# A two-stage kernel (decayed linear attention, then maxout): units of 256 tokens on 128 partitions, y made channel-first, and an order written out as a table

## The chip, the cores and the metric

The kernel runs on one core of a Trainium2 chip. The metric is device time in microseconds of that core; a kernel is run three times and the median counts.

## The reference

Four batches, eight heads, 768 tokens, 48 channels a head. A state of 48x48 a head is decayed by w and gains the outer product of k and v at each token; y reads it with r, with a bonus u for the token itself. The heads are then laid side by side (384 channels) and go through two products to 1024, an elementwise maximum, and a product back to 384. Everything is float32 at the boundary.

```python
for t in range(S):
    kt, vt, rt, wt = (k[:, :, t], v[:, :, t], r[:, :, t], w[:, :, t])
    cur = np.einsum('bhd,bhe->bhde', u[None] * kt, vt)
    y[:, :, t] = np.einsum('bhd,bhde->bhe', rt, state + cur)
    state = wt[:, :, :, None] * state + np.einsum('bhd,bhe->bhde', kt, vt)
...
x = np.ascontiguousarray(attn_out.transpose(0, 2, 1, 3)).reshape(B * S, H * D)
h1 = x @ w1
h2 = x @ w2
g = np.maximum(h1, h2)
return (g @ w_out).astype(np.float32)
```

## The kernel before

The tokens are cut into twelve units of 2 batches by 128 tokens. A unit's 64 token pairs of one batch lie on 64 partitions and those of the other batch on the other 64; the two tokens of a pair (index i) lie side by side along the free dimension. `load` brings w, k, r and v of a unit with eight transfers of 64 partitions (line 77), each piece 384 bytes long (2 tokens of 48 float32), into a pool of four buffers.

For each unit, `logw` takes the logarithm of w and adds the two tokens of a pair (POOL, line 172); `cumsum` makes the exclusive running sum over pairs with a product by a triangular matrix in float32 (line 198); `exps` gives the decay up to each token (A) and its inverse (iA); `scale_rk` multiplies r and k by them; `transp` turns both channel-first through TensorE (line 238) and copies them from PSUM on DVE (line 243). `scores` multiplies turned k by turned r in 64-row tiles (line 293) and a mask takes the causal half (line 296). `kv`, `decay` and `decay_exp` carry the state from one chunk to the next; the decay of the whole chunk makes a round trip through DRAM on ACT's queue (lines 216 and 224), because it has to change from the free dimension to partitions. `y_inter` adds the bonus (line 308) and the state's part (line 315), `y_intra` the chunk's own part (line 328). y comes out with tokens on partitions; `xt` turns it channel-first through TensorE (line 340).

The maxout is folded: max(h1, h2) = (h1 + h2)/2 + |h1 - h2|/2. `weights` makes wd = w1 - w2, and wc = (w1 + w2) @ w_out/2 once. `gate` computes x @ wd (line 352), ACT takes the absolute value (line 356), and `outp` adds x @ wc (line 364) and |x @ wd| @ w_out/2 (line 367), copies the 128x384 result (line 370) and sends it out on SP's queue (line 373) with a destination in which the pair index i is the outermost dimension.

The order is written out by hand in `step(a, t, m)`: in one step three units are in work, unit a in its sums and exponentials, unit t in its attention products, unit m in the maxout. The engines run their instructions in the order of issue. Ahead of step n, `load(n + 2)` is issued on SP, behind the two stores of the step before. The first three units and the weights come before the steady part.

## Time and profile before

| | us |
|---|---|
| median of 3 runs | 226.78 |
| the runs | 226.43 to 228.17 |
| span of the profiled execution | 226.8 |
| PE busy | 159.0 |
| DVE busy | 114.1 |
| POOL busy | 113.6 |
| ACT busy | 91.7 |

The profile was taken on one execution, and its span agrees with the median. 28.9 MB move through the DMA engines in it, nearly all on SP's queue. The profile names instructions by line: PE is TensorE's products, PEld its weight loads, SPq the issuing of transfers by SP. A "chain" is the work that ended last, followed back from the end of the span. A window row has, after its bounds and length, the busy time and count of PE, PEld, DVE, ACT and POOL, then the granted TensorE clock, the DMA share (1.00 is all 16 engines busy with one packet each, and packets overlap a little, so that it can be above 1), and GB/s. A chain row has the start, the length and what it is.

### The profile page before, as it was taken

What the parts mean: (1) busy time and instruction counts of PE and PEld (TensorE: products, weight loads), DVE (VectorE), ACT (ScalarE), POOL (GpSimd) and SP (SyncE); (2) the same over time, 40 slices, a digit from 0 to 9 for tenths busy, and PEclk for the clock granted to TensorE, in tenths of its full rate; (3) what the DMA queues carried; (4) which work ended last, traced back from release to release, by engine and by line L of the source; (5) the groups of instructions that cost most, each with busy time, mean ns of one, the idle gap of its engine ahead of it and who ended that gap; (6) DMA issues with size and microseconds to landing.
All of it is one profiled execution on the core that took longest, in us unless ns stands there. A gap on an engine that the chain in (4) does not pass through costs nothing.

```text
span 226.8 us, 5085 instructions
## 1 busy us (share of the span) xinstructions
PE 159.0 (70%) x2104; PEld 104.3 (46%) x2104; DVE 114.1 (50%) x135; ACT 91.7 (40%) x159; POOL 113.6 (50%) x118
## 2 busy tenths in 40 slices
PE   0216557195799848898839898378888398988910
PEld 0014444153576634666615656236556156665600
DVE  5166878710969490185840785802858405660000
ACT  2233113303765613464433556035644347344500
POOL 8494750004788828638549179086295494300000
PEclk9999999999999995899976999959999679999975
DMA  6979999990296439539584485385385811111110
GB/s 128 211 113 217 406 356 134 198 152 0 66 150 129 104 104 172 133 76 151 141 163 104 100 169 117 101 158 132 85 143 146 177 49 50 53 52 31 48 42 35
DMA packets 66254, 28.91 MB, mean 127 GB/s; under 512 B 61220, under 2 KB 65444, under 8 KB 66232
## 3 DMA queue, kind: packets, MB, share of 16 engines
q1 hardware_dynamic: 55792, 28.51, 55.0%
q10 hardware_dynamic: 10440, 0.08, 2.7%
q8 instruction: 16, 0.26, 0.5%
q14 instruction: 6, 0.05, 0.1%
HBM read 23.83 MB, written 4.76 MB: 126 GB/s over the span
## 4 chain that ended last, share of the span: by engine, by line
DMA 20%; PE 16%; SPq 8%; ACT 5%; issue 2%; DVE 1%; POOL 0%; ACTq 0%; DVEq 0%
DMA lw<-in_w_dram 20%; PE go L367 6%; SPq L77 6%; PE go L352 3%; PE go L364 3%; SPq L373 2%; ACT gT L356 2%; PE sc L293 1%; PE y L328 1%; ACT xT L342 1%; ACT osb L370 1%; ACT lw L170 1%; DVE kT L243 1%; PE y L315 1%; PE y L308 1%
## 5 line engine op out<-in xcount | busy, mean ns | idle before, releaser
L172 POOL TENSOR_TENSOR lp<-lw 128x384 f32<-128x384 f32 x12 | 12.3, 1022 | 60.5 <-ACT lw L170 39.5
L367 PE MATMUL go<-wo_sb,gT 128*128 128x384 bf16 x192 | 40.8, 362 | 0.0
L352 PE MATMUL go<-xT,wd_sb 128*128 128x256 bf16 x288 | 37.2, 273 | 2.5 <-ACT xT L342 1.5
L296 DVE TENSOR_TENSOR M<-sc,mask 128x1024 bf16<-128x1024 f32 x24 | 29.3, 1221 | 8.4 <-PE sc L293 8.4
L364 PE MATMUL go<-wc_sb,xT 128*128 128x384 bf16 x72 | 19.0, 381 | 18.7 <-ACT gT L356 18.7
L352 PEld LDWEIGHTS <-wd_sb 128*128 128x128 bf16 x288 | 26.9, 98 | 10.3 <-issue 5.5
L243 DVE COPY rT<-tr 128x1024 bf16<-128x1024 bf16 x12 | 8.3, 688 | 45.8 <-PE tr L238 45.8
L356 ACT ACTIVATE gT<-go 128x512 bf16<-128x512 f32 x48 | 27.3, 588 | 5.6 <-PE go L352 5.4
L370 ACT COPY osb<-go 128x384 f32<-128x384 f32 x24 | 11.5, 478 | 43.3 <-PE go L367 43.3
L367 PEld LDWEIGHTS <-gT 128*128 128x128 bf16 x192 | 20.7, 108 | 16.7 <-issue 6.7
L198 PE MATMUL ex<-lp,tri 128*128 128x384 f32 x24 | 12.1, 592 | 19.5 <-POOL lp L172 14.8
L180 POOL TENSOR_TENSOR rku<-rku,u_b 128x768 f32<-128x768 f32 x12 | 22.4, 1863 | 0.9
L179 POOL TENSOR_TENSOR rku<-lr,lk 128x768 f32<-128x768 f32 x12 | 22.4, 1868 | 0.0
L189 POOL TENSOR_TENSOR vd<-lv,dg 128x768 bf16<-128x768 f32 x12 | 17.7, 1474 | 9.1 <-DVE dg L187 8.3
L170 ACT ACTIVATE lw<-lw 128x768 f32<-128x768 f32 x12 | 10.1, 842 | 29.2 <-DMA lw<-in_w_dram 29.2
L203 DVE TENSOR_TENSOR mz<-ex,lw 128x384 f32<-128x384 f32 x12 | 6.7, 557 | 27.9 <-ACT A L202 27.9
L238 PE MATMUL tr<-ident,rkn 128*128 128x128 bf16 x192 | 16.3, 234 | 4.3 <-DVE rkn L230 3.0
L364 PEld LDWEIGHTS <-xT 128*128 128x128 bf16 x72 | 6.5, 105 | 23.0 <-issue 21.0
L238 PEld LDWEIGHTS <-rkn 128*128 128x128 bf16 x192 | 13.6, 105 | 7.0 <-DVE rkn L230 4.4
L231 DVE TENSOR_TENSOR rkn<-lk,iA 128x768 bf16<-128x768 f32 x12 | 16.0, 1333 | 0.0
L230 DVE TENSOR_TENSOR rkn<-lr,A 128x768 bf16<-128x768 f32 x12 | 15.5, 1293 | 0.3 <-ACT A L209 0.2
L333 ACT CAST x<-y 128x768 bf16<-128x768 f32 x12 | 9.6, 798 | 13.1 <-PE y L328 12.9
(56 smaller groups left out, 215.2 us busy)
## 6 DMA issues: line engine op xcount, KB each, us to landing
lw<-in_w_dram SPq DMA_DIRECT2D x24, 192.0 KB
lk<-in_k_dram SPq DMA_DIRECT2D x24, 192.0 KB
lr<-in_r_dram SPq DMA_DIRECT2D x24, 192.0 KB
lv<-in_v_dram SPq DMA_DIRECT2D x24, 192.0 KB
out_dram<-osb SPq DMA_DIRECT2D x24, 192.0 KB
w1f<-in_moe_w_dram SPq DMA_DIRECT2D x1, 1536.0 KB
w2f<-in_moe_w_dram SPq DMA_DIRECT2D x1, 1536.0 KB
wof<-in_moe_w_out_dram SPq DMA_DIRECT2D x1, 1536.0 KB
```

The lines of the kernel that those rows point to most:

```text
L179: nc.gpsimd.tensor_mul(rku, L[n]["r"], L[n]["k"])
L180: nc.gpsimd.tensor_mul(byi(rku), byi(rku), u_b.rearrange("p (h d) -> p h d", h=H).unsqueeze(1).to_broadcast([P, 2, H, D]))
L189: nc.gpsimd.tensor_mul(byi_inv(vd), L[n]["v"], dg.to_broadcast([P, H, 2, D]))
L230: nc.vector.tensor_mul(rkn[:, 0, :, :, 0:D], byi(L[n]["r"]), s["A"])
L231: nc.vector.tensor_mul(rkn[:, 1, :, :, 0:D], byi(L[n]["k"]), s["iA"])
L238: nc.tensor.transpose(tp[:, p, :, i, :], s["rkn"][:, x, i, 2 * p:2 * p + 2, :].rearrange("s r d -> s (r d)"), ident)
L296: nc.vector.tensor_mul(M.rearrange("s e p t -> s (e p) t"), sc.rearrange("s e p t -> s (e p) t"), mask[:, i].rearrange("s i q -> s (i q)") ...
L352: nc.tensor.matmul(g[:, f, :], wd_sb[:, ko, fo * P:(fo + 1) * P], s["xT"][:, ko].rearrange("p j t -> p (j t)"), start=(f == 0 and ko == 0) ...
L356: nc.scalar.activation(s["gT"][:, 2 * j:2 * j + 2].rearrange("p f j t -> p f (j t)"), g, AF.Abs)
L364: nc.tensor.matmul(o, s["xT"][:, ko, b, :], wc_sb[:, ko, :], start=(ko == 0), stop=False)
L367: nc.tensor.matmul(o, s["gT"][:, fo, b, :], wo_sb[:, fo, :], start=False, stop=(fo == FO - 1))
L370: nc.scalar.copy(osb, o)
```

## The change

The tokens are cut into segments of 256 tokens of one batch: 128 token pairs on 128 partitions. A unit is one or two batches of such a segment: two units of one batch first, then five of two batches, seven in all. One product by the triangle makes the running sum over all 128 pairs of a batch (line 272); w of a pair is multiplied before the logarithm (`wp`), so that one logarithm and one exponential a batch are taken, and the missing factor of w goes into r and k by multiplications (`rw`, `kw`). Scores are still made in tiles of 64 rows, q being the half of the 128 pairs; the state has two places, one for each half. y is made channel-first: the state, the values and the bonus are the stationary operands (lines 452, 464 and 474, the first two in pieces of 32 columns) and tokens run along the free dimension, so that y goes from PSUM straight to xT. The maxout is folded with a relu in place of the absolute value: wd = w1 - w2, wc = w2 @ w_out, max(h1, h2) = h2 + relu(h1 - h2). The gate's products have 512 columns where a unit has two batches. The row of decays makes its round trip on SP's queue. A 128x384 result goes out as two transfers of 64 rows. The weights come in ten pieces through five staging buffers. The loops are replaced by a table, ORDER, one word an operation; a letter after @ names the engine (a for ACT, d for DVE, p for POOL).

```diff
+UNITS = ((0, 1, 0), (1, 1, 0), (2, 2, 0), (0, 2, 1), (2, 2, 1), (0, 2, 2), (2, 2, 2))
...
+ORDER = """
+zero.v.0 tri load.0.w ident zero.m zero.r sel load.0.k zero.s.0 zero.k.1 mask load.0.r zero.v.1
+zero.v.2 u load.0.v zero.s.1 wp.0@d wload.1.0 zero.k.0 ln.0 wload.0.0 wload.1.1 ex.0 wload.0.1
+wload.1.2 rk.0.0@p mz.0 e0.0 ie.0 row.0 ru.0.0@p kw.0@d vb.0.0@a scale.0.1.0@d vb.0.1@p w2cast.0@p
+wdiff.0@d tr.0.1.0 w2turn.0 te.0.1.0@a dg.0 wload.0.2 w2cast.1@p woload.0 kv.0 w2take.0@d w2turn.1
+wdiff.1@d w2take.1@a vd.0.0@d wl.0 woload.1 woload.2 w2cast.2@d wdiff.2@d w2turn.2 wocast.0@p
+w2take.2@a rw.0@d woload.3 load.1.w scale.0.0.0@d we.0 st.0.0 tr.0.0.0 wocast.1@a load.1.k st.0.1
+...
+sc.3.0.0 te.3.1.1@a op.2.2 st.3.1 vd.3.0@p mk.3.0.0 load.5.r sb.3.0@a rk.4.0@p vd.3.1@d tr.3.0.1
+sb.3.1@a sc.3.0.1 op.2.0 te.3.0.1@a wl.4 rk.4.1@p we.3 oe.2.2@a mk.3.0.1 load.5.v sc.3.1.0 oe.2.0@a
+op.2.1 vb.4.0@a mk.3.1.0 ru.4.0@p vb.4.1@a sc.3.1.1 op.2.3 sm.3@d os.2.0 os.2.2 wp.5@p oe.2.1@d
+yi.3.0 oe.2.3@a mk.3.1.1 os.2.1 ya.3.0.0 we.4 ya.3.0.1 rw.4@p ln.5 yb.3.0 kw.4@d yi.3.1 xe.3.0@a
+ya.3.1.0 os.2.3 yb.3.1 ya.3.1.1 scale.4.0.0@p ex.5 xe.3.1@a vb.5.0@a ru.4.1@d load.6.w gt.3.0 e0.5
+vb.5.1@p tr.4.0.0 rl.3.0@a gt.3.1 scale.4.1.0@p te.4.0.0@d gt.3.2 rl.3.1@a mz.5 rl.3.2@a gt.3.3
+gt.3.4 rl.3.3@a scale.4.1.1@p dg.4 tr.4.1.0 rl.3.4@a gt.3.5 gt.3.6 scale.4.0.1@p ie.5 load.6.k
+rl.3.5@d tr.4.1.1 te.4.1.0@d rl.3.6@a gt.3.7 kv.4 te.4.1.1@a rl.3.7@d rk.5.0@p sc.4.0.0 st.4.0
+...
+mk.6.1.0 yi.6.0 yb.6.0 oe.5.1@d ya.6.0.1 ya.6.0.0 os.5.1 yi.6.1 xe.6.0@d yb.6.1 ya.6.1.1 ya.6.1.0
+op.5.2 xe.6.1@a gt.6.0 oe.5.2@a os.5.2 gt.6.1 rl.6.0@a rl.6.1@a gt.6.2 gt.6.3 rl.6.2@a rl.6.3@a
+gt.6.4 gt.6.5 rl.6.4@a rl.6.5@a gt.6.6 gt.6.7 rl.6.6@a rl.6.7@a op.5.3 op.6.2 oe.5.3@d os.5.3 op.6.0
+oe.6.2@a os.6.2 op.6.1 oe.6.0@a os.6.0 op.6.3 oe.6.1@d os.6.1 oe.6.3@a os.6.3
+""".split()
...
-    ldp = tc.alloc_tile_pool(name="ld", bufs=4)
+    def bank(dt, tag):
+        return ps.tile([P, 512 if dt is F32 else 1024], dt, tag=tag, name=tag, bufs=2)
+
+    def pair():
+        return ps.tile([P, 2, 512], F32, tag="Y", name="Y", bufs=2)
+    LD = {"w": 2, "k": 2, "r": 2, "v": 2}
...
+    def w_load(x, ko):
+        t = wt_([P, d_ff], F32, "wst", 5)
+        nc.sync.dma_start(out=t, in_=(moe_w1, moe_w2)[x][ko * P:(ko + 1) * P, :])
+        Z["w", x, ko] = t
+
+    def wo_load(a):
+        t = wt_([P, d_ff], F32, "wst", 5)
+        nc.sync.dma_start(
+            out=t[:, 0:2 * HD].rearrange("p (o n) -> p o n", o=2),
+            in_=moe_w_out[a * 2 * P:(a + 1) * 2 * P, :].rearrange("(o p) n -> p o n", p=P))
+        Z["wo", a] = t
+
+    def w_diff(ko, e="d"):
+        (nc.vector if e == "d" else nc.gpsimd).tensor_sub(wd_sb[:, ko, :], Z["w", 0, ko], Z["w", 1, ko])
+
...
+    def load(s, name):
+        src = {"w": w, "k": k, "r": r, "v": v}[name]
+        t = wt_([P, 2, H, 2, D], F32, "l" + name, LD[name])[:, 0:s.nb]
+        for b in range(s.nb):
+            nc.sync.dma_start(
+                out=t[:, b].rearrange("p h i d -> p h (i d)"),
+                in_=src[s.b0 + b, :, s.t0:s.t0 + SEG, :].rearrange("h (p i) d -> p h (i d)", i=2))
+        setattr(s, name, t)
...
+    def wp(s, e):
+        s.lg = wt_([P, 2, HD], F32, "lg", 2)[:, 0:s.nb]
+        mul(e, s.lg.rearrange("p b (h d) -> p (b h) d", h=H), tok(s.w, 0), tok(s.w, 1))
+
+    def ln(s):
+        nc.scalar.activation(s.lg, s.lg, AF.Ln)
+
+    def ex(s):
+        s.ex = pair()
+        for b in range(s.nb):
+            nc.tensor.matmul(s.ex[:, b, 0:HD], tri, s.lg[:, b])
+
+    def e0(s):
+        s.E = wt_([P, 2, HD], F32, "E", 2)[:, 0:s.nb]
+        nc.scalar.activation(s.E, s.ex[:, 0:s.nb, 0:HD], AF.Exp)
+
+    def mz(s):
+        s.mz = MZ[:, 0:s.nb]
+        for b in range(s.nb):
+            nc.vector.tensor_add(MZ[:, b, :, 0:D],
+                                 s.ex[:, b, 0:HD].rearrange("p (h d) -> p h d", h=H),
+                                 s.lg[:, b].rearrange("p (h d) -> p h d", h=H))
+
+    def ie(s):
+        s.iE = wt_([P, 2, HD], F32, "iE", 1)[:, 0:s.nb]
+        nc.scalar.activation(s.iE.rearrange("p b (h d) -> p (b h) d", h=H),
+                             s.mz.rearrange("p b h d -> p (b h) d")[:, :, 0:D], AF.Exp, scale=-1.0)
+
+    def row(s):
+        s.row = drp.tile([1, 2 * H * DP], F32, tag="row", name="row")[:, 0:s.nb * H * DP]
+        nc.sync.dma_start(out=s.row, in_=MZ[P - 1:P, 0:s.nb].rearrange("o b h d -> o (b h d)"))
+
+    def wl(s):
+        s.WL = wt_([P, 2 * NP], F32, "WL", 2)[:, 0:s.nb * NP]
+        nc.sync.dma_start(out=s.WL, in_=s.row.rearrange("o (a x) -> x (o a)", x=P))
...
+    def rw(s, e):
+        mul(e, tok(s.r, 1), tok(s.r, 1), tok(s.w, 0))
+
+    def kw(s, e):
+        mul(e, tok(s.k, 0), tok(s.k, 0), tok(s.w, 1))
+
+    def vb(s, x, e):
+        s.vp = vp_[s.n % len(vp_)][:, 0:s.nb]
+        copy(e, s.vp.rearrange("p b (q e) i d -> p e (b q) i d", e=2)[
+            :, x, :, :, x * (DP - D):x * (DP - D) + D],
+            s.v.rearrange("p b (q e) i d -> p e (b q) i d", e=2)[:, x])
...
+    def tr(s, x, b):
+        t = bank(BF16, "A")
+        setattr(s, f"tp{x}{b}", t)
+        for i in range(2):
+            for p in range(NP):
+                c = (i * NP + p) * P
+                nc.tensor.transpose(
+                    t[:, c:c + P],
+                    (s.kp if x else s.rp)[:, b, i, 2 * p:2 * p + 2, :].rearrange("s r d -> s (r d)"),
+                    identb)
...
+    def sc(s, b, j):
+        t = pair()
+        setattr(s, f"sc{b}{j}", t)
+        for p in range(NP):
+            for q in range(2):
+                for e in range(2):
+                    d = slice(e * DP, e * DP + D)
+                    nc.tensor.matmul(
+                        t[q * Q:(q + 1) * Q, e, p * P:(p + 1) * P].rearrange("s (i g) -> s i g", i=2),
+                        s.kT[d, b, j, p, q, :],
+                        s.rT[d, b, :, p, q, :], skip_group_check=True)
...
+    def into(s, b, q, r0, n):
+
+        o, c = r0 % P, r0 // P * P
+        new = not all((b, q, x) in s.begun for x in range(o, o + n, 32))
+        s.begun |= {(b, q, x) for x in range(o, o + n, 32)}
+        return dict(out=ytile(s, b)[o:o + n, q, c:c + P].rearrange("c (i g) -> c i g", i=2), start=new, stop=False,
+                    skip_group_check=True)
+
+    def yi(s, b):
+        for p in range(NP):
+            for q in range(2):
+                if s.c == 0 and q == 0:
+                    continue
+                for m in range(3):
+                    nc.tensor.matmul(
+                        lhsT=S_b[:, q, s.b0 + b, p].rearrange("d e c -> d (e c)")[
+                            :, m * 32:(m + 1) * 32],
+                        rhs=s.rT[:, b, :, p, q, :],
+                        **into(s, b, q, p * 96 + m * 32, 32))
+
+    def ya(s, b, j):
+        for e in range(2):
+            for p in range(NP):
+                for m in range(2):
+                    for q in range(2):
+                        g = slice(q * Q, (q + 1) * Q)
+                        nc.tensor.matmul(
+                            lhsT=s.vp[g, b, 2 * p + e, j, m * 32:(m + 1) * 32],
+                            rhs=s.M[b, j][g, e, p, :].rearrange("s (i g) -> s i g", i=2),
+                            **into(s, b, q, p * 96 + (e + m) * 32, 32))
+
+    def yb(s, b):
+        for i in range(2):
+            for ko in range(KO):
+                for q in range(2):
+                    g = slice(q * Q, (q + 1) * Q)
+                    nc.tensor.matmul(
+                        lhsT=s.vd[g, b, i].rearrange("p h d -> p (h d)")[:, ko * P:(ko + 1) * P],
+                        rhs=sel[g, i],
+                        **into(s, b, q, ko * P, P))
+
+    def xe(s, b, e):
+        if b == 0:
+            s.xT = wt_([P, 4, KO, P], BF16, "xT", 2)
+        copy(e, s.xT[:, 2 * b:2 * b + 2].rearrange("c q k t -> c q (k t)"), s.y[b][:, :, 0:HD])
...
+    def gt(s, f):
+        t = bank(F32, "G")
+        setattr(s, f"g{f}", t)
+        n = 2 * s.nb
+        for m in range(2 // s.nb):
+            for ko in range(KO):
+                fo = f * 2 // s.nb + m
+                nc.tensor.matmul(
+                    t[:, m * n * P:(m + 1) * n * P].rearrange("c (b t) -> c b t", t=P),
+                    wd_sb[:, ko, fo * P:(fo + 1) * P], s.xT[:, 0:n, ko, :],
+                    start=(m == 0 and ko == 0), stop=(ko == KO - 1), skip_group_check=True)
+
+    def rl(s, f, e):
+        if f == 0:
+            s.gT = wt_([P, FO * 4 * P], BF16, "gT", 2)
+        o, i = s.gT[:, f * 4 * P:(f + 1) * 4 * P], getattr(s, f"g{f}")
+        if e == "a":
+            nc.scalar.activation(o, i, AF.Relu)
+        else:
+            nc.vector.tensor_scalar_max(o, i, 0.0)
...
-        osb = wt_([P, HD], F32, "osb", 4)
-        nc.scalar.copy(osb, o)
-        tok = (b0 + b) * S + c * C
-        dst = out[tok:tok + C, :].rearrange("(q i) n -> i q n", i=2)
-        nc.sync.dma_start(out=dst, in_=osb)
+    def os(s, a):
+        t = getattr(s, f"os{a}")
+        t0 = (s.b0 + a // 2) * S + s.t0 + (a % 2) * P
+        dst = out[t0:t0 + P, :].rearrange("(g i) n -> g i n", i=2)
+        for i in range(2):
+            nc.sync.dma_start(out=dst[:, i, :], in_=t[i * Q:(i + 1) * Q])
...
-    logw(0)
-    step(0, None, None)
-    load(3)
-    step(1, 0, None, ahead=False)
-    step(None, 1, None)
-    weights()
-    logw(2)
-    load(4)
-    step(2, None, 0)
-    for n in range(3, NU + 2):
-        if n + 2 < NU:
-            load(n + 2)
-        step(n if n < NU else None, n - 1 if n - 1 < NU else None, n - 2)
+    for o in ORDER:
+        o, _, e = o.partition("@")
+        name, *a = o.split(".")
+        a = [int(x) if x.isdigit() else x for x in a] + ([e] if e else [])
+        if name in ops:
+            ops[name](*a)
+        else:
+            unit[name](U[a[0]], *a[1:])
```

## The prediction

> **What bounds the kernel now.** I read the page first (busy shares, slices, chain), then the windows around one stall, then the chain piece by piece, for the period and for the price of each group of products.

> ```profile
> PE 159.0 (70%) x2104; PEld 104.3 (46%) x2104; DVE 114.1 (50%) x135; ACT 91.7 (40%) x159; POOL 113.6 (50%) x118
> DMA  6979999990296439539584485385385811111110
> DMA 20%; PE 16%; SPq 8%; ACT 5%; issue 2%; DVE 1%; POOL 0%; ACTq 0%; DVEq 0%
> ```

> No engine is over 70% busy, and the chain's largest item is a transfer, the load of w. The last slices show transfers at a tenth of the DMA engines, when only output leaves.

> ```profile
> 101.50:104.50 3.00, 3.00 (x49) 1.80 (x48) 2.91 (x3) 1.28 (x2) 2.85 (x3) 1.00 1.19 230
> 120.50:122.00 1.50, 1.50 (x36) 0.89 (x35) 0.00 (x0) 0.73 (x2) 1.50 (x3) 0.50 0.13 50
> 217.00:225.00 8.00, 0.00 (x0) 0.00 (x0) 0.00 (x0) 0.00 (x0) 0.00 (x0) 0.59 0.13 46
> 23.00:28.00 5.00, 2.92 (x58) 2.01 (x57) 4.26 (x4) 0.80 (x1) 4.14 (x3) 1.00 1.02 409
> 93.60:105.50 11.90, 11.21 (x182) 7.69 (x180) 8.46 (x10) 7.12 (x14) 6.17 (x6) 1.00 0.67 134
> ```

> The last two columns are the DMA share and GB/s. Loads alone (first line) use all 16 engines, 230 GB/s. Output alone (third line) has a share of 0.13, which is 2.1 of 16 engines, and 46 GB/s; the second line is the same thing in mid-run, while the next unit's w is waited for. So line 373 writes through two engines: its destination is two rows deep on the outside (2x64x384). One output tile of 196,608 B takes 196.6/46 = 4.3 us there, two a step 8.5 us; the same two engines also carry their part of a step's loads, 1.57 MB at 230 GB/s = 6.8 us. Together 15.4 us. The period of the steps is in the chain:

> ```profile
> 98.13 1.42 PE go L352 x12
> 99.54 0.35 PE sc L293 x16
> 99.89 0.43 PE y L308 x4
> 100.33 0.45 PE y L315 x8
> 101.42 1.30 PE go L367 x8
> 102.72 0.52 PE y L328 x32
> 107.08 8.65 DMA lw<-in_w_dram
> ...
> 169.31 8.53 DMA lw<-in_w_dram
> ...
> 187.34 0.90 PE ex L198 x2
> ...
> 193.51 0.49 PE go L364 x3
> ...
> 199.78 0.46 PE tr L238 x8
> ```

> The w load that is waited for comes every (169.31 - 107.08)/4 = 15.6 us (four steps lie between), the 15.4 just worked out. A step that does not wait takes 11.9 us (the fifth window, PE busy 11.2 of it). So each step gives about 3.7 us to two overloaded DMA engines, ten steps some 35 us, and the last two tiles leave 8.5 us of tail.

> **The change, part by part.** *Stores.* Each tile leaves as two transfers of 64 rows, as each load of line 77 now has 64 rows, and those loads show all 16 engines. At 230 to 409 GB/s the two tiles of 256 tokens then take 1.0 to 1.7 us in place of 8.5. All transfers sum to 18.9 MB/0.23 = 82, weights 4.7/0.409 = 11.5, stores 12 to 20: about 110 us, below any finish I consider, so DMA stops being the bound after the start. Twice as many stores cost SP 24 more issues of 0.5 us (its rows in the queue's waits), which nothing waits for while loads run a unit ahead.

> [...]

> *PE, for 256 tokens.* Before, from the chain's rows: gate 2x1.42, output 2x(0.49+1.30), turning r and k 2x0.46, cumulative sum 0.90, scores 0.42+0.35, y 0.43+0.45+0.52, keys by values 0.44 and turning x 0.50 (both from the timeline): 11.35 us, 95% of the 11.9. After: gate the same (half the products, twice the columns); turning x goes (-0.50), since y comes out channel-first. In exchange, line 464 makes 64 products of 64 rows by 32 columns over 128 tokens instead of 32 over 48, and line 452 makes 20 of 32 columns instead of 8. No row has 32-column tiles. The nearest is line 293, 128 columns on four quarter tiles: 16 in 0.35, 22 ns each, so 64 take 1.4 (+0.9) and 20 take 0.44 (no change). Sum 11.75. Bounds: eight tiles at once, half of 1.4, gives 11.05; no overlap at all is the 57 ns of a 128-column turn (0.46/8), 84x57 = 4.8 for both, which gives 14.7. I take 11.75, because lines 293 and 328 both overlap partial tiles.

> [...]

> *The other engines.* Sums over the order table at the rows' means: ACT about 94 us (it gives up a copy of x and gains most copies of turned r and k, 17 at 0.80 to 1.07 by line 342, plus casts of v from POOL), DVE about 110 (one sum of mz instead of two; masks stay 24x1.22), POOL about 106. They are nearly what they were, and for 512 tokens POOL has about 19 us (two rk at 1.87, one or two ru at 1.86, two vd at 1.47, three or four scale at 1.47, kw 1.87, wp 2.0) against PE's 23.5. They are hidden as long as POOL's 1.87 holds.

> *Row and decay loads* move from ACT's queue to SP's, five pairs. Before, the row left at 11.59 and its return was issued at 15.66, so a wait is some 4 us, and stores and loads are queued behind it. Loads already in the queues (up to a unit, 6.8 us for 256 tokens) cover it; uncovered, five would cost 20 us of transfers, of which DMA has 80 to spare.

> *Start.* Before, the first gate product was at 55.9. After: first unit 2 + 6.8 = 9, weights 11.5 to 21, about 3 for staging (five buffers, freed by DVE's 1.22 us differences), second unit to 31. Its r lands at 29, and POOL then does rk 1.87, kw 1.0, vb 0.4, two scale at 1.47: 35. A turn, and the first gate product at 38.

> *Sum.* Twelve times 11.75 is 141; 6.7 of it lies before the first gate product (the first unit's attention 5.3, the second's sum 0.90 and turn 0.46), leaving 134. At 94% (before's 95%, a point off for POOL) 143 us. The third unit is loaded in full only at about 45 and the fifth's w at about 67, where PE arrives at nearly the same time and in-order engines wait on v and w: 5 us. End: copy 0.48 and a spread store, 4 (before 9.9 after its last copy, 8.5 of it the two tiles). 38 + 143 + 5 + 4 = **190 us**. This is against the profiled span of 226.8, the same as the median 226.78.

> **Rivals.** *A. Forecast, 0.68:* PE is the bound, 175 to 199. The low end is 11.05 a unit and no early wait: 38 + 126/0.95 + 4.

> *B. POOL and hand-offs set the pitch, 0.19:* POOL's line 179 took 2.52 us at 12.08 while DVE ran beside it, 1.35 times its mean. At that POOL has 25.5 for 512 tokens instead of 19, and with one wait for it a unit the pitch is 28 instead of 25. Over four such units that is +12: 202, and 212 if the start slips too. For: sixteen of POOL's operations a unit stand in front of turns. Against: the mean over both cases is 1.87.

> *C. 32-column tiles do not overlap, 0.09, slower:* at 57 ns the sum is 2.95 up a unit, times 11.4 over 0.94: +36, 226. If their weight loads (104 ns in the PEld groups) do not hide either, 84x0.104 = 8.7, +83, 273; the middle is 245. It decides from 60 ns a product. Against: no partial tile in this trace behaves so.

> *D. The stores stay on two engines, 0.04:* 12x15.4 + 11.5 + 2 = 198 if those engines never idle, with the present idling up to 226; about 222. Against: the loads' share.

> **Numbers.** A measurement tells from no change what differs by about 1%, 2.3 us. A and B are faster; C is slower but for its lowest corner; D is mostly faster or the same. Faster 0.88, same 0.03, slower 0.09. The range takes A and B: 175 to 212.

> **What would show it.** Stores at a DMA share near 1 or short bursts instead of a floor of 0.13; no "DMA lw" in the chain beyond the first 70 us; PE at 75% or more; the first gate product (line 491) at 36 to 42; 64 products of line 464 in 1.2 to 1.7 us; a period of 23 to 27 us for 512 tokens; under 5 us after the last copy. A line 464 group above 3.6 us, a period above 28 with PE idle for POOL, or a w wait in each unit would make it wrong.

## The result and the profile after

The kernel after takes 175.56 us (median; 175.24 to 179.63) where the kernel before took 227.22 in the same series: 0.7712 of it, 95% interval 0.7679 to 0.7745. Some executions of a kernel run a few us longer than its others (here the one of 179.63); ratios are made without them, so a median need not equal a ratio times 227. The profiled execution has a span of 174.1 us.

The page's busy shares, its DMA slices, the first line of its chain, and one line of its DMA issues (the last number is the us from issue to landing):

```profile
PE 144.7 (83%) x2552; PEld 87.7 (50%) x2552; DVE 113.8 (65%) x126; ACT 90.2 (52%) x140; POOL 116.0 (67%) x86
...
DMA  5999999999999967798763914501013100211143
...
PE 53%; DVE 6%; issue 3%; ACT 0%
...
out_dram<-osb SPq DMA_DIRECT2D x48, 96.0 KB, 2.2
```

The transfers now come first and, up to about 61 us, almost without a break. The chain can be followed back to 62.7 us; no transfer is in it, and PE carries 53% of the span. A store of 64 rows lands 2.2 us after its issue. The first product of the gate, from the timeline of PE:

```profile
33.39 1.47 PE L491 MATMUL G<-xT,wd_sb 128*128 128x256 bf16 x12 [0.33 <-ACT xT L143]
```

The chain, from the part where PE is its only carrier (from 74.3 on; from 62.7 to there it is mostly DVE); first one stretch of the two-batch unit, then two places where it breaks:

```profile
80.21 1.30 PE G L513 x8
81.51 0.35 PE Y L421 x16
...
85.48 0.46 PE Y L452 x24
85.94 0.35 PE Y L464 x32
86.29 0.44 PE Y L474 x12
86.73 0.30 PE Y L464 x21
87.03 1.45 issue
88.48 0.29 PE Y L464 x11
88.78 2.44 PE Y L272 x4
91.22 1.28 PE G L491 x3
...
94.38 1.45 PE G L491 x6
95.83 0.45 PE A L351 x8
96.28 1.29 PE G L491 x6
...
108.52 0.33 PE Y L474 x7
108.85 2.54 issue
111.39 0.34 PE Y L474 x5
```

"issue" at 87.03 and 108.85 is time in which PE waited for nothing that the profile shows, each time in the middle of a group of small products (21 of 32 and 7 of 12 were done). The windows of the loads' stretch and around these places (after the bounds and the length: PE, PEld, DVE, ACT, POOL, the granted clock, the DMA share, GB/s):

```profile
33.39:62.00 28.61, 24.84 (x448) 16.67 (x455) 22.81 (x28) 19.75 (x30) 19.88 (x12) 0.94 1.00 259
...
84.00:90.00 6.00, 4.55 (x195) 3.18 (x184) 3.38 (x2) 3.08 (x6) 5.92 (x5) 0.93 0.56 145
90.00:96.00 6.00, 5.96 (x31) 2.75 (x31) 2.92 (x4) 3.69 (x7) 5.12 (x3) 0.78 0.59 158
...
102.00:108.00 6.00, 6.00 (x182) 3.83 (x170) 4.92 (x5) 3.06 (x5) 5.92 (x4) 1.00 0.33 76
108.00:114.00 6.00, 3.46 (x108) 2.08 (x96) 2.54 (x1) 1.44 (x2) 6.00 (x4) 0.92 0.56 159
114.00:120.00 6.00, 6.00 (x25) 2.89 (x24) 0.44 (x1) 3.02 (x6) 3.20 (x2) 0.79 0.14 33
162.00:168.00 6.00, 6.00 (x39) 3.62 (x37) 0.56 (x1) 0.96 (x2) 0.00 (x0) 1.00 0.29 72
```

After each break a window of 6 us has a mean clock of 0.78 or 0.79. In the trace that is half the clock for 3.4 us, from 89.17 to 92.58 and from 113.06 to 116.48, with the full clock on both sides. In the windows up to 114 us POOL is busy nearly without a gap, and outside the two breaks PE is full beside it.

Between three marks, in us, the two profiled executions and that of the first experiment (the kernel before with nothing but its stores spread) divide like this:

| | before | before, stores spread | after |
|---|---|---|---|
| start to the first product of the gate | 55.9 | 55.4 | 33.4 |
| from there to the start of the last output copy | 160.6 | 138.7 | 136.4 |
| from there to the end | 10.3 | 4.5 | 4.3 |
| span | 226.8 | 198.6 | 174.1 |

By these marks 28 us come with the spread stores, 22 with the start, and 2.5 with all that changed in the attention, the maxout and their order. The first mark does not stand at the same amount of work, though. The kernel before has done the attention of two units of 256 tokens by then (its turns of line 340 for both come before 38 us), the kernel after that of one, and PE is busy 127.9 us between the two marks in after and 123.2 in the kernel with spread stores. At the 5.3 us that the prediction gave a unit's attention, an estimate, the split is rather 17 for the start and 8 for the rest.

### The profile page after: what moved, and what is told of

The parts are those of the page before. It is cut to its first block, busy times and chain, and to the rows that moved or that the text cites. A ratio compares the mean times of both kernels' runs of the same rounds, so it can differ in the third digit from the quotient of the medians.

```text
span 174.1 us, 5787 instructions
## 1 busy us (share of the span) xinstructions
PE 144.7 (83%) x2552; PEld 87.7 (50%) x2552; DVE 113.8 (65%) x126; ACT 90.2 (52%) x140; POOL 116.0 (67%) x86
## 4 chain that ended last, share of the span: by engine, by line
PE 53%; DVE 6%; issue 3%; ACT 0%
PE G L513 16%; PE G L491 13%; PE G L509 6%; PE A L351 3%; PE Y L464 3%; PE Y L421 3%; PE Y L474 2%; PE Y L272 2%; PE Y L452 2%; DVE lr L147 2%; DVE S_f L147 1%; PE Y L383 1%; DVE dg L313 1%; DVE rku L147 1%; DVE MZ L281 1%
## 5 line engine op out<-in xcount | busy, mean ns | idle before, releaser
L491 PE MATMUL G<-xT,wd_sb 128*128 128x512 bf16 (+1 forms) x168 | 37.1, 357 | 0.8 <-ACT xT L143 0.7
L513 PE MATMUL G<-wo_sb,gT 128*128 128x384 bf16 x192 | 37.3, 340 | 0.0
L428 DVE TENSOR_TENSOR M<-Y,mask 128x1024 bf16<-128x1024 f32 x24 | 28.6, 1218 | 5.1 <-PE Y L421 5.0
L501 ACT ACTIVATE gT<-G 128x512 bf16<-128x512 f32 x40 | 23.8, 597 | 7.4 <-PE G L491 6.5
L491 PEld LDWEIGHTS <-wd_sb 128*128 128x128 bf16 x168 | 16.1, 100 | 16.1 <-issue 6.2
L147 POOL TENSOR_TENSOR rp<-lr,E 128x768 bf16<-128x768 f32 x9 | 17.5, 1954 | 7.7 <-ACT gT L501 7.0
L147 POOL TENSOR_TENSOR vd<-lv,dg 128x768 bf16<-128x768 f32 x10 | 14.7, 1473 | 7.2 <-DVE dg L313 7.2
L272 PE MATMUL Y<-lg,tri 128*128 128x384 f32 x24 | 11.4, 596 | 8.3 <-ACT lg L267 5.9
L147 POOL TENSOR_TENSOR kp<-lk,iE 128x768 bf16<-128x768 f32 x8 | 16.6, 2088 | 0.2
L509 PE MATMUL G<-wc_sb,xT 128*128 128x384 bf16 x72 | 16.3, 336 | 0.0
L147 POOL TENSOR_TENSOR rku<-rku,u_b 128x768 f32<-128x768 f32 x8 | 15.1, 1885 | 1.7 <-DVE rku L147 0.9
L313 DVE TENSOR_REDUCE dg<-rku 128x32 f32<-128x1536 f32 (+1 forms) x7 | 10.6, 1515 | 0.0
```

Of the source, the lines that this page charges most:

```text
L147: (nc.vector if e == "d" else nc.gpsimd).tensor_mul(o, a, b)
L272: nc.tensor.matmul(s.ex[:, b, 0:HD], tri, s.lg[:, b])
L313: nc.vector.reduce_sum(s.dg.rearrange("p b h o -> p (b h) o"), s.rku.rearrange("p b h i d -> p (b h i) d"), axis=AX.X)
L428: nc.vector.tensor_mul(t.rearrange("s e p t -> s (e p) t"), getattr(s, f"sc{b}{j}").rearrange("s e (p t) -> s (e p) t", p=NP), mask[:, j]. ...
L491: nc.tensor.matmul(t[:, m * n * P:(m + 1) * n * P].rearrange("c (b t) -> c b t", t=P), wd_sb[:, ko, fo * P:(fo + 1) * P], s.xT[:, 0:n, ko, :],
L501: nc.scalar.activation(o, i, AF.Relu)
```

## The experiments

**The stores alone, both ways.** In the kernel before:

```diff
-        nc.sync.dma_start(out=dst, in_=osb)
+        for i in range(2):
+            nc.sync.dma_start(out=dst[i], in_=osb[i * Q:(i + 1) * Q])
```

> The kernel before, with line 373's store split into two of 64 rows, nothing else. Theory S (stores): the two overloaded DMA engines set the period of 15.6 us; freed, a step takes its own 11.9, ten steps give back some 35 us and the tail 8: 180 to 195 us. Rival R (units and order): the wait for w moves to the next thing that is late and the gain came from the new units and order: over 215.

Measured: 200.94 us (198.72 to 203.11), ratio 0.8817 [0.8753, 0.8881]. From the page:

```profile
PE 149.0 (75%) x2104; PEld 101.0 (51%) x2104; DVE 117.2 (59%) x135; ACT 91.7 (46%) x159; POOL 117.8 (59%) x118
...
DMA  5997999899009593695954876959359596030303
```

That lies between the two expectations: theory S holds in kind, at a smaller size. The floor of one tenth at the end is gone, and the tail is 4.5 us where it was 10.3. A step now takes 12.6 us (eight steps from 74.05 to 175.18 by the turns of line 340) where the waits for w had made it 15.6. The stores are worth 26 us, not the 43 that the prediction gave them: by the same turns only seven steps gained, from 111.3 us in all (74.51 to 185.81) to 89.4 (74.05 to 163.45), 3.1 a step in place of 3.7 for ten steps; what comes before and after them takes the same in both kernels; and the tail gave 5.8 of the 8.5.

In the kernel after, the opposite edit, one store of 2x64x384 a tile:

```diff
-        dst = out[t0:t0 + P, :].rearrange("(g i) n -> g i n", i=2)
-        for i in range(2):
-            nc.sync.dma_start(out=dst[:, i, :], in_=t[i * Q:(i + 1) * Q])
+        dst = out[t0:t0 + P, :].rearrange("(g i) n -> i g n", i=2)
+        nc.sync.dma_start(out=dst, in_=t)
```

> The changed kernel, with each result tile stored by one transfer to a 2x64x384 destination as before. S: two DMA engines carry 12 x 15.4 + 11.5 of weights + 2 = 198 us of transfers, so 198 to 212. R: the deeper loads hide it, under 182.

Measured: 192.21 us (190.77 to 193.37), ratio 0.8444 [0.8393, 0.8495]: 16.6 us more than after, between the two expectations. A window of its end:

```profile
180.00:190.00 10.00, 0.00 (x0) 0.00 (x0) 0.00 (x0) 0.00 (x0) 0.00 (x0) 0.50 0.13 50
```

The floor is back, and the tail is most of the price: from the start of the last output copy (175.1) to the end of the span (191.7) it is 12.3 us longer than in after. The rest lies in the middle, where the chain has one wait that after has not, 10.01 us for the row of decays to leave (its transfer, on the same queue as the stores, lands only at 78.27). Between the marks this kernel lost 5 us where the kernel before had lost 22. That its loads run further ahead, and so absorb most of their delay, fits this but was not tried by itself.

**The start.** The kernel before with spread stores, and with the weights' transfers ahead of the second unit's:

```diff
-    load(1)
...
+    load(1)
...
-    step(0, None, None)
-    load(3)
-    step(1, 0, None, ahead=False)
-    step(None, 1, None)
+    step(0, None, None, ahead=False)
+    step(None, 0, None)
+    logw(1)
     weights()
...
+    load(3)
+    step(1, None, None, ahead=False)
...
-    step(2, None, 0)
+    step(2, 1, 0)
```

> The kernel before with its stores split, and its start rearranged: the weights are loaded before the second unit, the first unit's attention and the weights are worked before the second unit's sums. With the stores alone it took 200.9, and its first gate product came at about 55. If the start explains what the stores leave of the gain, the first gate product comes at about 40 and the time is 183 to 190. If the rest of the gain lies in the units and the table, it stays above 196.

Measured: 196.45 us (195.72 to 199.52), ratio 0.8651 [0.8591, 0.8711]. The first product of the gate came only at 49.85. The second unit's sums (line 198) waited behind the weights' products on PE (line 157's group alone took 5.76), the turn of its r and k then waited for DVE (2.78), and the third unit's sums, which stand ahead of the gate, waited for POOL's line 172 (3.61). So the edit did not make the start that it was meant to make, and the time is only just above 196. Still, the mark came 5.5 us earlier and the span is 4.8 shorter: the end kept most of it. That the other 16 us of after's start come from its smaller first units and ten weight pieces was not tried piece by piece.

**The order.** The kernel after with its operations, from the first product of the gate on, in the plain order of a step (all loads of a unit, then sums, turns, scores, y and output one after the other):

```diff
-scale.1.0.0@p ru.1.0@d ya.0.0.1 wctake.0@a xe.0.0@a load.2.v scale.1.1.0@p tr.1.0.0 gt.0.0
-te.1.0.0@a dg.1 gt.0.1 rl.0.0@d vd.1.0@p kv.1 wl.1 tr.1.1.0 load.3.w st.1.0 rl.0.1@a gt.0.2 st.1.1
...
+scale.1.0.0@p ru.1.0@d ya.0.0.1 wctake.0@a xe.0.0@a load.2.v scale.1.1.0@p tr.1.0.0 dg.1 vd.1.0@p
+load.3.w load.3.k load.3.r load.3.v wl.1 te.1.0.0@a wp.2@d ln.2 ex.2 e0.2 mz.2 gt.0.0 rl.0.0@d
...
```

> The changed kernel from the first gate product on in a plain order: the step of the kernel before (turn, gate, sums, scores, output, y), with the same engine for each operation; the start and all functions as in the changed kernel. If the table's order matters beyond the stores: 187 to 205, with PE waiting on POOL and on w. If it is only the stores and the units: under 182.

Measured: 212.19 us (210.88 to 213.52), ratio 0.9345 [0.929, 0.9401], outside both expectations: 36.6 us more than after. Two lines of its page, and the longest of SP's waits (us in total, times, the longest):

```profile
PE   0353792968493993929994829985949999999991
...
DMA  6999999898896018960116990113000212031123
```

```profile
SPq L526 <- ACT osb L143: 85.8, 16, 19.9
```

PE and the transfers now go in bursts: SP stands for up to 19.9 us at a store whose output copy is not made yet, and the loads of the next unit are queued behind it. The new operations in this order are slower than the old ones with spread stores. This is one plain order among many, so 36.6 is the price of this one, and not a figure for tables in general.

**POOL.** Line 309 (the bonus multiplied by u on POOL and DVE) left out; it is part of the computation.

```diff
-        mul(e, t, t, u_b.rearrange("p (h d) -> p h d", h=H).unsqueeze(2).to_broadcast([P, H, 2, D]))
+        return
```

> The changed kernel without the multiplication by u in the bonus (line 309), so the bonus is as if u were one. That takes 15.1 us from POOL and 7.5 from DVE. PE-bound (A): no more than 4 us less, 171 to 176. POOL sets the pitch (B): 6 or more less, under 169.

Measured: 172.24 us (171.12 to 173.5), ratio 0.7586 [0.754, 0.7632]. From the page, and PE's waits (us in total, times, the longest):

```profile
PE 141.6 (84%) x2552; PEld 87.1 (51%) x2552; DVE 100.2 (59%) x122; ACT 90.1 (53%) x140; POOL 97.9 (58%) x78
```

```profile
PE Y L474 <- issue: 2.5, 1, 2.5
...
PE Y L464 <- issue: 1.2, 1, 1.2
```

18 us less on POOL and 13.6 less on DVE brought 3.3: POOL does not set the pitch. The two breaks of PE stayed where they were.

**The small products, doubled.** Line 464's products issued twice (the chunk's own part then counts double in y):

```diff
-        for e in range(2):
+        for e in (0, 0, 1, 1):
```

> The changed kernel with every product of line 464 issued twice, so the chunk's own part of y is counted twice. 768 more products: at the 11 ns that the trace shows (32 in 0.35) they add 8.4 us of PE. If PE is the bound (A) the time rises by 6 to 10, to 182 to 186. If POOL sets the pitch (B) it rises by under 4. If the instruction supply is what stopped PE in the middle of two such groups, 98 KB more of instructions bring more such stops: over 187.

Measured: 193.72 us (193.54 to 193.76), ratio 0.853 [0.8501, 0.856]: 18.2 us more. The products' group on the page, then their lines in the chain around one place:

```profile
L464 PE MATMUL Y<-M,vp 64*32 64x128 bf16 x1536 | 18.1, 220 | 11.7 <-issue 11.7
```

```profile
117.10 0.46 PE Y L452 x24
117.56 1.21 PE Y L464 x112
118.76 2.58 issue
...
122.02 0.68 PE Y L464 x58
123.48 1.31 issue
```

The group grew from 9.9 to 18.1 us, 8.2 for 768 more products, 11 ns each. Most of the rest is time in which PE stood for "issue", 13.1 us (11.7 of it in this group) in place of 4.0. The time is that of the third expectation. The seven longest breaks within groups came at PE's instructions number 1985, 3009, 3265, 4033, 4289, 5313 and 6337, counted from its first; the two of after at 2497 and 3265. All are 193 plus a multiple of 256. The instruction queue of the two pages (packets, MB, share), first after's, then this kernel's:

```profile
q8 instruction: 20, 0.33, 0.8%
...
q8 instruction: 26, 0.43, 0.9%
```

A packet has 16.4 KB (0.33 MB / 20), and PE's instructions number 5115 and 6651: in both kernels one packet for every 256 of them (20 and 26 packets), 64 bytes an instruction (16.4 KB / 256). A block of 256 is 128 weight loads and 128 products, and at 11 ns a product it lasts 1.4 us, while one packet of that queue took 0.9 to 1.6. In after, at 108.85, a packet started at 109.09, ended at 110.10, and PE went on at 111.39. The traces hold the times of every packet. In all nine breaks the instruction that PE stood for is the 193rd after 256 times n, and PE went on 1.26 to 1.58 us after the n-th packet had ended (the 9th for instruction 2497, the 12th for 3265). In the two traces, and in that of the next experiment, no such instruction ran sooner after its packet than that, and wherever the packet had ended 1.6 us or more ahead there was no break. So, by these times, PE ran out of instructions in all nine. What the last 1.3 us are, and what decides when a packet starts, is open.

**The small products, spaced.** If that is so, it is enough to set longer products between the groups of small ones. In the table, two groups of output products (op.2.3 and op.3.3) are moved in between:

```diff
-op.2.1 vb.4.0@a mk.3.1.0 ru.4.0@p vb.4.1@a sc.3.1.1 op.2.3 sm.3@d os.2.0 os.2.2 wp.5@p oe.2.1@d
-yi.3.0 oe.2.3@a mk.3.1.1 os.2.1 ya.3.0.0 we.4 ya.3.0.1 rw.4@p ln.5 yb.3.0 kw.4@d yi.3.1 xe.3.0@a
-ya.3.1.0 os.2.3 yb.3.1 ya.3.1.1 scale.4.0.0@p ex.5 xe.3.1@a vb.5.0@a ru.4.1@d load.6.w gt.3.0 e0.5
...
-mk.4.1.0 op.3.1 ru.5.0@p sb.4.1@a os.3.0 mk.4.0.1 sc.4.1.1 vd.4.1@p oe.3.1@a op.3.3 sm.4@d os.3.1
-wp.6@p load.6.v mk.4.1.1 yi.4.0 oe.3.3@a ya.4.0.1 ya.4.0.0 yi.4.1 ya.4.1.0 rk.5.1@p ln.6 yb.4.1
...
+sc.3.1.0 oe.2.0@a op.2.1 vb.4.0@a mk.3.1.0 ru.4.0@p vb.4.1@a sc.3.1.1 sm.3@d os.2.0 os.2.2 wp.5@p
+oe.2.1@d yi.3.0 mk.3.1.1 os.2.1 ya.3.0.0 we.4 ya.3.0.1 rw.4@p ln.5 yb.3.0 op.2.3 oe.2.3@a kw.4@d
+yi.3.1 xe.3.0@a ya.3.1.0 yb.3.1 os.2.3 ya.3.1.1 scale.4.0.0@p ex.5 xe.3.1@a vb.5.0@a ru.4.1@d
...
+oe.3.1@a sm.4@d os.3.1 wp.6@p load.6.v mk.4.1.1 yi.4.0 ya.4.0.1 ya.4.0.0 op.3.3 oe.3.3@a yi.4.1
```

> The changed kernel with two words of the table moved: in the fourth and fifth units one group of output products (11 long ones) is put between the groups of short products of y instead of ahead of them. PE stopped there for 1.45 and 2.54 us in the middle of a group, at the 193rd instruction of a block of 256 both times, waiting for no semaphore. If that is the supply of instructions (16 KB a fetch), the stops shrink and with them the slow clock behind: 168 to 172.5. If it is something else, the same time within 1 us.

Measured: 169.62 us (166.88 to 172.09), ratio 0.7408 [0.7355, 0.746]; a second series, beside the last experiment below:

> The spaced order by itself, once more on the chip of the run beside it, so that the two can be compared: 168 to 171, no stop of PE over 0.6 us after 64 us in the profile, and the granted clock above 0.98.

It gave 168.45 us (167.53 to 171.55), ratio 0.7426 [0.7386, 0.7465]. This version beats both kernels. From its page, and windows of it with the columns as above:

```profile
PE 141.0 (85%) x2552; PEld 86.3 (52%) x2552; DVE 113.8 (68%) x126; ACT 90.3 (54%) x140; POOL 116.4 (70%) x86
...
PEclk9999999999699999999999999999999999999999
```

```profile
78.00:90.00 12.00, 11.98 (x280) 7.20 (x278) 9.57 (x9) 7.61 (x14) 11.92 (x7) 1.00 0.81 205
90.00:102.00 12.00, 11.96 (x240) 7.15 (x246) 10.29 (x14) 8.27 (x12) 12.00 (x8) 1.00 0.70 184
102.00:114.00 12.00, 12.00 (x234) 7.36 (x219) 6.56 (x7) 7.24 (x11) 11.92 (x6) 1.00 0.44 117
```

Both breaks are gone, and with them the low clock behind them: from 44.28 us to the end of the work the clock is full. The margin is small: at the two places PE's instruction comes 1.67 and 1.78 us after its packet. The first product of the gate is where it was (33.32), the last output copy 7.5 us earlier. The chain of after adds up to that: the breaks took 1.45 + 2.54 = 4.0, and the groups behind them took longer than their like elsewhere, line 272's x4 2.44 for 1.29, line 491's x3 1.28 for 0.65, line 513's x8 2.48 for 1.30, line 491's x6 1.79 for 1.29, together 3.5.

**The rows of decays.** In after, lines 292 and 296 on ACT's queue, as before the change; then the same in the spaced order:

```diff
-        nc.sync.dma_start(out=s.row, ...)
+        nc.scalar.dma_start(out=s.row, ...)
...
-        nc.sync.dma_start(out=s.WL, ...)
+        nc.scalar.dma_start(out=s.WL, ...)
```

> The changed kernel with the ten row and decay transfers issued on ACT's queue, as before. The prediction held that their move to SP costs nothing: 174 to 177. If SP's waits on them hold back loads, ACT's queue gives 2 us or more. If the wait for a row's landing now stops ACT, it is over 178.

> The spaced order of the table (the third and fourth output products of units 2 and 3 set between groups of small products) together with the row and decay loads on ACT's queue instead of SP's. If the two gains are of separate things they add: 175.6 - 6 - 1.7 = 168, range 165.5 to 169. If the rows' gain was only that loads came a little earlier at a place where PE then stopped for instructions anyway, or was chance, the time is that of the spaced order alone, 169 to 170.5.

Measured in after: 173.85 us, from four executions of 171.05, 171.55, 176.15 and 179.04; its ratio is 0.7543 [0.749, 0.7596]. In the spaced order: 170.91 us (168.27 to 171.55), without a ratio, against 168.45 for the spaced order alone. So once the breaks are gone ACT's queue gains nothing, and in the trace of after SP stood at lines 292 and 296 for 3.9 us in all, 0.7 of it for a row to land. What made two executions 4 us shorter than after in the first case is open: the profiled one is that of 179.04, and it had both breaks.

## Why the prediction was right, and where it was not

The forecast, PE as the bound, held from 74 us on; 190 was 14 too long. That 175.56 still lies in the range, at its very foot of 175, is luck: the start and the products were both cheaper than the sum had them, and the two breaks, which no step of the prediction had, put 7.5 us back. Without them the same operations take 168.45, below the range.

- **Two engines for the stores: right in kind, too dear in size.** "Ten steps some 35 us" and 8.5 of tail were 26 in all (28 by the spans). Rival D's "198 or more" fell to 192 on the chip: it priced the loads at 230 GB/s, and after's window from 33.4 to 62, with a DMA share of 1.00, has 259. That takes 12 x 0.7 = 9 us off the bound, which is enough; it was not tried by itself.
- **Start, 38: measured 33.4.** The second unit's loads came sooner: POOL multiplied r by k of that unit at 26.69, where the prediction had the loads of r land at 29 and POOL begin after that. The two slices of the page in which that unit comes (21.8 to 30.5 us) have 320 and 271 GB/s, where the prediction took 230 for it.
- **11.75 us of products for 256 tokens: too high, the term that was off most.** The 64 products of line 464 took 0.70 (11 ns each; 32 in 0.35 in the chain) and not 1.4: the spacing of the prediction's low bound, half of the 22 ns of line 293, was the fact. That line, taken for the nearest, has tiles of 64 columns and kept its 22 ns in after (line 421, 16 in 0.35 in the chain); those of line 464 have 32. The gate with 512 columns took 2.58 (two of the chain's 1.29) and not 2.84. Line 452's 20 took 0.38 (24 in 0.46) for 0.44. Together 1.02 less, so 10.73, under even the low bound of 11.05; 11.6 us over 11.4 units (some 0.5 less, since the first two units keep 256 columns): 134 becomes 122.4 to 122.9, and the spaced order, without breaks, spent 124.3 there.
- **The allowance for idle time, 9 + 5: measured 8.6, of another kind.** PE idled 3.8 from 33 to 62 and 0.7 from there to 74, mostly the early waits; the other 4.0 are the two breaks for instructions, which no step of the prediction had. They also cost clock, so that PE was busy 127.9 and not 124.3 as in the spaced order.
- **Rival B: its premise came true and its price did not.** DVE and POOL took longer side by side (DVE 2.62 at 63.84 for 0.95 at 49.92, POOL 2.59 at 106.85 for 1.82 at 42.16), and POOL was busy 5.9 of 6 us from 66 to 84. But from 74 on the chain is PE, and 18 us off POOL with 13.6 off DVE gave 3.3. From 62.7 to 74.3 the chain does run over DVE and its waits, and PE stood for only 0.7 us of that.
- **C and the end:** line 464's products came every 11 ns and line 452's every 19 (24 in 0.46), under the 60 from which C decides, so C fell; the end took 4.3 for the 4 predicted. The sum by its steps: start -4.6, products -6.1, idle time -5.4, end +0.3, of 190; the span of 174.1 is left, to 0.1.

What the prediction did not ask is where the gain would be without the change's core. By the marks, spread stores and the start make 50 of the 52.7 us of the spans, and the new y, scores and maxout 2.5 (8 if the unit's attention that the start leaves over is counted), and only in the table's order; 7.5 more when the breaks are taken out.

## What to carry to other kernels

Read the share and the GB/s of a stretch with only one kind of transfer in it before anything else: one edit of three lines gave half of what this rewrite did. When products become smaller and more numerous, price them by a spacing measured on tiles of their own shape (here 11 ns on 64 by 32, where line 421, with 64 columns, had 22), and count weight loads and products in a row: here some hundred pairs at 11 ns outran the supply of instructions, and one group of eleven long products between them was the cure, with little to spare. The sign here was an "issue" break within a group, at instruction numbers that differ by multiples of 256.

## What the runs showed of the hardware

```profile
49.92 0.95 DVE L147 TENSOR_TENSOR lr<-lr,lw 128x768 f32<-128x768 f32 x1
63.84 2.62 DVE L147 TENSOR_TENSOR lr<-lr,lw 128x768 f32<-128x768 f32 x1
106.80 0.96 DVE L147 TENSOR_TENSOR lr<-lr,lw 128x768 f32<-128x768 f32 x1 [0.57 <-POOL rku L147]
```

```profile
51.02 1.82 POOL L147 TENSOR_TENSOR rp<-lr,E 128x768 bf16<-128x768 f32 x1 [7.04 <-ACT gT L501]
...
63.83 1.82 POOL L147 TENSOR_TENSOR rku<-rku,u_b 128x768 f32<-128x768 f32 x1 [0.89 <-DVE rku L147]
...
106.85 2.59 POOL L147 TENSOR_TENSOR lk<-lk,lw 128x768 f32<-128x768 f32 x1
```

At 49.92 POOL was idle, and DVE took 0.95. At 63.84 DVE started 0.01 us after POOL and took 2.62, close to 0.95 and POOL's 1.82 together, while POOL took no more than its 1.82. At 106.85 POOL started 0.05 us after DVE and took 2.59, against 1.82 for the same multiplication at 42.16, while DVE took 0.96. In both places the one that started second took longer; the cause was not tried.
